# A new order of issue on every engine, without pace waits, in a fused attention, memory and MoE kernel

## The chip, the cores and the metric

One core of a Trainium2 chip runs the kernel. Its engines are TensorE (PE in the profile; PEld is its loading of weights), VectorE (DVE), ScalarE (ACT), GpSimd (POOL) and SyncE (SP, which here issues nearly all transfers). The metric is the device time of one execution in microseconds; lower is better.

## The reference

```python
B, H, S, D = (4, 8, 576, 64);  n_tokens, d_model, d_ff = (2304, 512, 1536)
scores = where(causal, -1e9, q @ k.T / sqrt(D))
a = exp(scores - max);  a /= a.sum(-1) + 1e-09
local = a @ v
q_p = phi(q)                      # phi(x) = elu(x) + 1
mem_out = (q_p @ M_prev) / (q_p @ z_prev + 1e-06)
x = sigmoid(beta) * mem_out + (1 - sigmoid(beta)) * local
xn = x / sqrt(mean(x * x) + 1e-06) * rms_g
out = (silu(xn @ w_gate) * (xn @ w_val)) @ w_out
```

The weights of the MoE part come as 8-byte floats. Products run on float16 halves (a high and a low part of each operand, three products for one), except for the first rows, which run in float32.

## The kernel before

**Tiles.** The 2304 tokens are 18 blocks of 128 rows: blocks 0 to 3 are the first of each batch (in float32, "32" in their names), then four or so full ones per batch, and two tail blocks (9 and 17) that hold the last 64 rows of two batches each. Nine chunks of two blocks go through the MoE part: `m_proj` (L1068) makes gv, the gate and value products, `m_act` and `m_split` make the hidden half-floats, `m_down` (L1142) adds into out.

**A unit of attention** is one block and a group of heads: `u_scores` (scores sc, their maxima nm and S on DVE, in one instruction for each), exp on ACT, `u_exp`'s high half of P on ACT, `u_lo` (L678) the low half on DVE and its transposing transfer PT on SP, then `u_pv` (L699), the product with v into loc. Tail blocks do the same on column halves (`tail_scores`, `tail_pv`). `x_norm` (L873) squares the finished rows x on ACT and takes the power on POOL, `x_float` (L884) and `x_split` (L899) bring x transposed into xT for gv.

**The head.** Weights (`load_w`, pieces 0 to 23) come in over SP and are converted from 8-byte floats by `f64_to_f32` (L988): two instructions on ACT (L992, L996), one on DVE (L1002). `gram` (L265) makes sums csum of k, v and of the weights, from which scales follow. gv of chunk 0 needs x0, x1 and the converted pieces.

**What sets the order.** The program is written out in Python by step lists, but the order in which each engine issues is set at the end by `issue_in_order` (L193). Each helper carries a letter (`@keep`), and its instructions are sorted into a lane for each engine and letter. `ISSUE` (L62 to 130) has one string for each of PE, ACT, DVE, POOL and SP: a letter takes the next instruction of that lane, a number behind it that many, `~k` the one k places further on. Each engine issues strictly in that order; an instruction whose operands are not ready holds all that stand behind it, and SP's transfers are issued one after the other likewise. Tiles come from pools with a fixed number of buffers, so a transfer into a pool's buffer waits until the readers of the tile that had it are done.

**Pace waits.** Besides the waits that the data need, the kernel sets waits with no data behind them (`after`, L697): the first product of each csum waits for the norm of x0 or x1 (`GDE`), the loads of kv4, kv10, kv5 and of the pre tiles for that of x1 (`GDL`), the copies for the second pair's memory likewise, the loads of w_out for earlier conversions (`paced`, L923), and both ACT instructions of pieces 2 to 11 wait for `e11`, POOL's last addition of x1 (`CDP`, `CDE`).

Of the kernel before, what the change touches and what calls it, by code (L numbers as in the profile page):

```python
# [31 lines left out]
GDE = ("x0", "x1")  # L32
GDL = ("x1", "x1")
LAG0 = 8
NA = 4
# [11 lines left out]
XP = 4  # L47
XB = 0
HLB = 5
RING = 5  # L50
PACE = 4
EARLY = 8
HTAG = ("v16", "v16", "v16", "v16")
CDP = (2, 12)
CDE = "e11"
# [78 lines left out]
def attn_memory_moe_kernel(  # L134
# [198 lines left out]
    @keep("l")  # L333
    def load_kv(n, ev=""):
# [60 lines left out]
    def stat_blk(b, i):  # L395
        if b < 2:
# [353 lines left out]
    def pair_memory(pr):  # L750
# [98 lines left out]
    def loc_evac(n, g4):  # L849
# [666 lines left out]
```

## Time and profile before

| | |
|---|---|
| runs | 627.65, 633.29, 633.80 us (median 633.29) |
| the profiled execution | 625.11 us |
| its span, from first to last instruction | 623.4 us |
| mean granted TensorE clock | 0.989 |
| PE busy | 590.9 us (95%), 6124 instructions |
| DVE, ACT, POOL busy | 433.0, 396.4, 132.9 us |
| the longest groups on PE | gv L1086 306.1, out L1160 to L1162 200.1, sc L604 78.1, gv L1079 47.5 us |
| moved by DMA | 87.57 MB, 140 GB/s on average |

Busy time is summed over the span, and matmuls overlap in the pipeline. A row of the timeline gives an instruction's start and duration; in brackets stands how long the engine had been idle before it and what released it. [...]

### The profile page before, as it was taken

Reading aid. Unit: us, or ns where it says so; the run is one execution under the profiler, and the core shown is the slowest. Engines: PE = TensorE matmul, PEld = TensorE weight load, DVE = VectorE, ACT = ScalarE, POOL = GpSimd, SP = SyncE. Lnnn points to the kernel's source line nnn. Section 1 sums busy time; section 2 is a strip of 40 time slices with the busy share of each in tenths; the row PEclk is TensorE's granted clock in tenths of the full one; section 3 lists DMA queues with packets and bytes.
Section 4 is the critical chain, followed back from the end, with each engine's and each line's share of the span. In section 5 each row is a group of like instructions: output and inputs, shape, how many; then the busy total and the mean of one; then the engine's idle time right before and its main releaser. Section 6 shows DMA issues by size and latency. Waiting matters only on the chain. (4 is left out here: it accounts for less than half of the span.)

```text
span 623.4 us, 15863 instructions
## 1 busy us (share of the span) xinstructions
PE 590.9 (95%) x6124; PEld 458.6 (74%) x6124; DVE 433.0 (69%) x1271; ACT 396.4 (64%) x856; POOL 132.9 (21%) x221
## 2 busy tenths in 40 slices
PE   5789999999999999999998999999999999989996
PEld 4768886677767888877766667777787787767774
DVE  3767689899999778776864677796876855632221
ACT  4687587998987757676565665975775644532221
POOL 2320001124332222121221221122222212121111
PEclk9979999999999999999999989999999999989999
DMA  7996246579769687885587279559996434620001
GB/s 259 359 388 262 86 148 207 144 175 201 159 99 195 132 170 121 190 156 93 74 202 118 58 161 163 133 99 155 158 152 117 87 68 99 100 44 18 34 1 35
DMA packets 183787, 87.57 MB, mean 140 GB/s; under 512 B 165792, under 2 KB 165792, under 8 KB 183712
## 3 DMA queue, kind: packets, MB, share of 16 engines
q1 hardware_dynamic: 180640, 81.82, 60.6%
q10 hardware_dynamic: 3072, 4.74, 2.5%
q8 instruction: 48, 0.79, 0.5%
q14 instruction: 27, 0.22, 0.1%
HBM read 37.77 MB, written 4.72 MB: 68 GB/s over the span
## 5 line engine op out<-in xcount | busy, mean ns | idle before, releaser
L1086 PE MATMUL gv<-xT,wgv 128*128 128x256 f16 x2304 | 306.1, 274 | 1.9 <-DMA xT<-x 1.6
L1086 PEld LDWEIGHTS <-wgv 128*128 128x128 f16 x2304 | 220.7, 98 | 44.8 <-issue 3.5
L1125 POOL TENSOR_TENSOR h<-th,h 128x256 f16<-128x256 f32 x88 | 64.2, 729 | 287.6 <-ACT h L1124 283.5
L667 ACT ACTIVATE S<-S,nm 128x256 f32<-128x256 f32 (+3 forms) x112 | 70.5, 640 | 51.4 <-DVE nm L610 32.3
L686 DVE SCALAR_TENSOR_TENSOR P<-S,P 128x512 f16<-128x512 f32 (+2 forms) x96 | 67.4, 704 | 31.0 <-ACT P L184 30.7
L1104 DVE SCALAR_TENSOR_TENSOR th<-th,gv 128x256 f32<-128x256 f32 x96 | 39.7, 414 | 63.5 <-ACT th L1103 63.3
L604 PE MATMUL sc<-kT,qT 128*128 128x128 f16 x576 | 78.1, 219 | 5.4 <-DMA kT<-row 2.0
L1103 ACT ACTIVATE th<-gv,wt 128x256 f32<-128x256 f32 x96 | 44.5, 463 | 44.2 <-PE gv L1086 39.5
L610 DVE CUSTOM_DVE_ANT_0 S<-sc,mask,qsc 128x256 f32<-128x256 f32 (+2 forms) x96 | 57.3, 610 | 19.8 <-PE sc L604 19.4
L1161 PE MATMUL out<-wo,h 128*128 128x512 f16 x176 | 67.0, 381 | 0.0
L1162 PE MATMUL out<-wo,h 128*128 128x512 f16 x176 | 66.6, 381 | 0.0
L1160 PE MATMUL out<-wo,h 128*128 128x512 f16 x176 | 66.5, 381 | 0.0
L184 ACT ACTIVATE P<-S 128x512 f16<-128x512 f32 (+2 forms) x96 | 57.8, 604 | 11.5 <-DMA PT<-P 10.8
L1124 ACT CAST h<-th 128x256 f16<-128x256 f32 x88 | 35.1, 399 | 42.8 <-DVE th L1107 38.4
L604 PEld LDWEIGHTS <-qT 128*128 128x128 f16 x576 | 48.2, 98 | 11.2 <-issue 6.9
L1079 PE MATMUL gv<-xT,wgv 128*128 128x256 f32 x192 | 47.5, 398 | 0.8 <-DVE xT L895 0.8
L1107 DVE SCALAR_TENSOR_TENSOR th<-th,wt,gv 128x256 f32<-128x256 f32 x96 | 45.7, 476 | 1.7
L724 PE MATMUL loc<-v,PT 128*128 128x65 f16 x288 | 41.1, 193 | 3.9 <-DVE t L844 1.9
L1079 PEld LDWEIGHTS gv<-xT,wgv 128*128 128x128 f32 x192 | 37.0, 199 | 8.1 <-issue 1.9
L726 PE MATMUL loc<-v,PT 128*128 128x65 f16 x288 | 41.3, 192 | 0.0
L725 PE MATMUL loc<-v,PT 128*128 128x64 f16 x288 | 40.8, 194 | 0.0
L724 PEld LDWEIGHTS <-PT 128*128 128x128 f16 x288 | 27.4, 97 | 8.4 <-DMA PT<-P 3.1
(231 smaller groups left out, 1004.6 us busy)
## 6 DMA issues: line engine op xcount, KB each, us to landing
kv<-in_qkv_dram SPq DMA_DIRECT2D x40, 256.0 KB, 3.9
q<-in_qkv_dram SPq DMA_DIRECT2D x18, 256.0 KB, 3.6
wo<-in_moe_w_out_dram SPq DMA_DIRECT2D x8, 512.0 KB, 4.0
out_dram<-res ACTq DMA_DIRECT2D x16, 256.0 KB, 2.9
wgv<-in_moe_w_val_dram SPq DMA_DIRECT2D x7, 512.0 KB, 9.2
wo<-in_moe_w_gate_dram SPq DMA_DIRECT2D x7, 512.0 KB, 8.0
qT<-qT SPq DMA_DIRECT2D x28, 128.0 KB, 2.7
wgv<-in_moe_w_gate_dram SPq DMA_DIRECT2D x5, 512.0 KB, 7.5
```

The lines of the kernel that those rows point to most:

```text
L184: got = fn(*p, **k)
L604: nc.tensor.matmul(t[:, g * w + j * P : g * w + (j + 1) * P], qT[n][:, t2, h, :], kT[blk_of[(b, j)]][:, h, :], start=(t2 == 0), stop=(t2 = ...
L610: nc.vector.tensor_tensor_reduce(out=s[:, g * w : (g + 1) * w], in0=t[:, g * w : (g + 1) * w], in1=mask[:, m0 : m0 + w], scale=qsc[n][:, 5 ...
L667: nc.scalar.activation(v_, v_, AF.Exp, bias=nm[:, g : g + 1], scale=-1.0)
L686: m = nc.vector.scalar_tensor_tensor(out=p16[:, w : 2 * w], in0=s[:, :w], scalar=PSCALE, in1=p16[:, :w], op0=ALU.mult, op1=ALU.subtract)
L724: nc.tensor.matmul(a, phi_, vhi, start=(j == 0), stop=False)
L1079: nc.tensor.matmul(o, wgv[:, 1 + p, o0 : o0 + P], xT[0][:, cc, at], start=(cc == 0), stop=(cc == NC - 1))
L1086: nc.tensor.matmul(o, lhs, xT[c][:, rhs, :], start=(cnt == 0), stop=(cnt == 3 * NC - 1))
L1125: nc.gpsimd.tensor_tensor(h16[:, 1], th, h16[:, 0], ALU.subtract)
L1160: nc.tensor.matmul(o, hh, whi, start=(f == 0), stop=False)
L1161: nc.tensor.matmul(o, hh, wlo, start=False, stop=False)
L1162: nc.tensor.matmul(o, hl, whi, start=False, stop=(f == NF - 1))
```

## The change

The five strings of `ISSUE` are replaced throughout, and the pace waits go with their names. No instruction is added, removed or changed: both programs issue the same 5878 products, the same transfers and the same operations on DVE, ACT and POOL. The products of the tail blocks stand on column halves in both. Of the strings a line each stands here.

```diff
-GDE = ("x0", "x1")
-GDL = ("x1", "x1")
...
-XP = 4
-XB = 0
...
-PACE = 4
...
-CDP = (2, 12)
-CDE = "e11"
...
-        "T8ZZ~1T8ZT4SS~1S~2S~3Zu4T4S5S~1S~2S~3T4S4u2Tu2Th4T4u4~4T2hTh3T2u4Th8ss~3ss~2ss~1s2R8G4G4~4GG~3GZG~2G3Z~1GZT4ZT4"
+        "T8ZZ~1T4ZT4SS~1S~2S~3ZT4u3T4S4TSS~1S~2S~3T3uS4T2u4h4T2u4~4T3h4T~1Tu4T3h4s2s2~2ss~1s2h4R4ss4~3s3R4ZG4G4~4G8T4Z~1Z"
...
-    def gram(acc, src, first, last, ev=""):
+    def gram(acc, src, first, last):
...
-            m = nc.tensor.matmul(acc[:, :P], w, w, start=first and g == 0, stop=last and g == 3)
-            if g == 0 and ev:
-                after(m, event[ev])
+            nc.tensor.matmul(acc[:, :P], w, w, start=first and g == 0, stop=last and g == 3)
...
-            ins = nc.sync.dma_start(out=stage[n][:, j], in_=qkv[at_row[n], :, j, :])
-            if ev:
-                after(ins, event[ev])
+            nc.sync.dma_start(out=stage[n][:, j], in_=qkv[at_row[n], :, j, :])
...
-            if b > 1:
-                after(m, event['x1'])
...
-        if p - PACE in begun:
-            tc.add_manual_dep(
-                ins.ins, begun[p - PACE].ins.name,
...
-        begun[p] = nc.scalar.activation(dst, r[:, :, 1], AF.Prelu, scale=2.0 ** -112, alpha=2.0 ** 32)
-        late = CDP[0] <= p < CDP[1]
-        if late:
-            after(begun[p], event[CDE])
...
+        nc.scalar.activation(dst, r[:, :, 1], AF.Prelu, scale=2.0 ** -112, alpha=2.0 ** 32)
```

Line numbers of the program after are lower: L950 and L951 there are L992 and L996 here, L379 is L387, L469 is L477, L684 is L692, L623 is L631, L678 is L686.

**ACT in the head,** about 25 us in. junk_369 is the square of x0, junk_401 that of x1; S with den are exponentials, wgv_84 the conversions of weights, ph_542 the first step of phi for block 2. Before:

```order
L659 ACTIVATE S_295,den_308<-S_295,nm_296 128x128 x4
L387 ACTIVATE junk_369,xs_368<-t1_0_326 128x512
L387 ACTIVATE junk_401,xs_400<-t1_1_341 128x512
L509 ACTIVATE ph_542<-q2_198 128x512
L992 ACTIVATE wgv_84<-wgv_84 128x512
L996 ACTIVATE wgv_84<-wgv_84 128x512
```

After:

```order
L651 ACTIVATE S_295,den_308<-S_295,nm_296 128x128 x4
L379 ACTIVATE junk_369,xs_368<-t1_0_326 128x512
L950 ACTIVATE wgv_84<-wgv_84 128x512 x2
L951 ACTIVATE wgv_84<-wgv_84 128x512
L950 ACTIVATE wgv_84<-wgv_84 128x512
L379 ACTIVATE junk_401,xs_400<-t1_1_341 128x512
L379 ACTIVATE junk_468,ssm0_467<-wo_85 128x512
L950 ACTIVATE wgv_84<-wgv_84 128x512
```

Four instructions of three conversions stand now between the two squares, and ph_542 comes after more of them (below the piece).

**SP around kT11,** about 320 us in. PT are transposes of probabilities for the product with v, kT and phT those of keys and of phi(q), q and kv are loads. Before:

```order
L692 DMA_TRANSPOSE PT_5128<-P16_5004 128x10x128
L477 DMA_TRANSPOSE phT11_5188<-row16_5185 128x8x128
L338 DMA kv3_5301<-in_qkv_dram 128x512
L382 DMA q13_5717<-in_qkv_dram 128x512
L692 DMA_TRANSPOSE PT_5265<-P16_5131 128x10x128
L477 DMA_TRANSPOSE kT11_4959<-row16_4956 128x8x128
L692 DMA_TRANSPOSE PT_5330<-P16_5268 128x10x128
L692 DMA_TRANSPOSE PT_5446<-P16_5334 128x8x128
```

After:

```order
L494 DMA qT11_4737<-qT11_4737 64x1024
L469 DMA_TRANSPOSE kT11_4959<-row16_4956 128x8x128
L684 DMA_TRANSPOSE PT_5128<-P16_5004 128x10x128
L684 DMA_TRANSPOSE PT_5265<-P16_5131 128x10x128
L374 DMA q12_5207<-in_qkv_dram 128x512
L469 DMA_TRANSPOSE phT11_5188<-row16_5185 128x8x128
L684 DMA_TRANSPOSE PT_5330<-P16_5268 128x10x128
L684 DMA_TRANSPOSE PT_5446<-P16_5334 128x8x128
```

kT11_4959 went from behind PT_5128, phT11, two loads and PT_5265 to a place ahead of them; the loads of kv3 now stand earlier, outside the piece.

**DVE in the last attention unit,** about 545 us in. S_9117 takes scores sc_9119 and sct_9137 and their maximum nm_9118; P16 rows make the low half of the probabilities, th rows are the MoE part, fl and t2 finish attention rows. Before:

```order
L686 SCALAR_TENSOR_TENSOR P16_9070<-S_9024,P16_9070 128x640
L631 ISA S_9117,nm_9118<-sc_9119,mask_67,qsc_7898 128x512
L631 ISA nm_9118 128x1
L858 SCALAR_TENSOR_TENSOR fl_9112<-loc17_0_8788,tcb3_6421 128x4
L641 ISA S_9117,nm_9118<-sct_9137,tmask_78,nm_9118,qsc_7898 128x128
L641 ISA nm_9118 128x1
L861 RECIPROCAL fl_9112<-fl_9112 128x4
L1104 SCALAR_TENSOR_TENSOR th_8781<-th_8781,gv91_8727 128x256
L862 TENSOR_TENSOR t2_17_9111<-loc17_0_8788,fl_9112 128x256
L1107 SCALAR_TENSOR_TENSOR th_8781<-th_8781,wt_90,gv91_8727 128x256
L686 SCALAR_TENSOR_TENSOR P16_9160<-S_9117,P16_9160 128x640
```

After:

```order
L623 ISA S_9117,nm_9118<-sc_9119,mask_67,qsc_7898 128x512
L623 ISA nm_9118 128x1
L633 ISA S_9117,nm_9118<-sct_9137,tmask_78,nm_9118,qsc_7898 128x128
L633 ISA nm_9118 128x1
L839 SCALAR_TENSOR_TENSOR fl_9112<-loc17_0_8788,tcb3_6421 128x4
L842 RECIPROCAL fl_9112<-fl_9112 128x4
L678 SCALAR_TENSOR_TENSOR P16_9070<-S_9024,P16_9070 128x640
L678 SCALAR_TENSOR_TENSOR P16_9160<-S_9117,P16_9160 128x640
```

Both rows of S_9117 now stand ahead of P16_9070, and the two P16 rows stand together.

## Rows read from the trace of the kernel before

**Rows 1.** The page, part 1: busy us of each engine, share of the span, instructions.
```profile
PE 590.9 (95%) x6124; PEld 458.6 (74%) x6124; DVE 433.0 (69%) x1271; ACT 396.4 (64%) x856; POOL 132.9 (21%) x221
```

**Rows 2.** Waits of PE: line, releaser, us in total, times, longest us.
```profile
PE tp L527 <- DMA kv<-in_qkv_dram: 5.8, 1, 5.8
...
PE loc L739 <- DMA PT<-P: 2.7, 1, 2.7
...
PE loc L724 <- DVE t L844: 1.9, 1, 1.9
PE loc L724 <- DMA PT<-P: 1.7, 3, 0.7
...
PE gv L1086 <- DMA xT<-x: 1.6, 2, 1.1
...
PE csum L271 <- DVE wgv L1002: 0.2, 1, 0.2
```

**Rows 3.** Stretches: length; busy us (instructions) by engine; clock, DMA share, GB/s.
```profile
32.43:39.26 6.83, 6.05 (x18) 4.85 (x18) 4.45 (x7) 6.83 (x15) 2.56 (x5) 0.50 1.03 393
360.11:363.52 3.41, 3.41 (x16) 1.79 (x13) 1.70 (x4) 1.64 (x4) 1.35 (x2) 0.50 1.06 134
554.67:558.08 3.41, 3.15 (x41) 2.46 (x42) 0.77 (x3) 0.40 (x1) 0.72 (x1) 0.50 0.00 0
...
334.50:338.00 3.50, 3.50 (x60) 2.89 (x60) 1.79 (x8) 1.93 (x5) 0.00 (x0) 1.00 0.10 21
...
150.00:200.00 50.00, 47.93 (x520) 37.03 (x519) 49.76 (x141) 40.40 (x86) 15.95 (x24) 1.00 0.82 151
```

**Rows 4.** Timeline of the head: start us, us, instruction, idle time before it.
```profile
26.68 1.10 PE L804 MATMUL loc<-kv,PT 128*128 128x64 f32 x8 [0.76 <-DVE t L820]
...
27.02 0.74 DVE L891 TENSOR_SCALAR diag<-ident,xs 128x128 f32<-128x128 f32 x1 [0.40 <-POOL xs L880]
...
27.62 0.62 PE L271 MATMUL csum<-kv 128*128 128x128 bf16 x8
...
29.08 0.63 ACT L387 ACTIVATE junk<-t 128x512 bf16<-128x512 f32 x1 [3.02 <-POOL t L822]
...
30.93 1.05 DVE L891 TENSOR_SCALAR diag<-ident,xs 128x128 f32<-128x128 f32 x1
...
32.03 1.75 PE L894 MATMUL xtp<-diag,t 128*128 128x128 f32 x8 [2.85 <-DVE ph L511]
...
34.56 7.32 PE L1079 MATMUL gv<-xT,wgv 128*128 128x256 f32 x22 [0.78 <-DVE xT L895]
```

**Rows 5.** Two stretches of the head, and loads of w_val (page, part 6).
```profile
0.00:20.00 20.00, 12.86 (x83) 10.58 (x83) 9.69 (x58) 11.33 (x32) 4.52 (x20) 1.00 0.83 294
20.00:30.00 10.00, 8.42 (x80) 8.09 (x79) 7.86 (x30) 5.17 (x24) 3.74 (x7) 1.00 1.05 346
...
wgv<-in_moe_w_val_dram SPq DMA_DIRECT2D x7, 512.0 KB, 9.2
```

**Rows 6.** Timeline, 325 to 335 us: SP's issues and two waits of PE.
```profile
325.84 1.38 SPq L692 DMA_TRANSPOSE PT<-P  x1
...
327.63 1.53 SPq L477 DMA_TRANSPOSE kT<-row  x1
...
328.07 0.32 PE L604 MATMUL sc<-kT,qT 128*128 128x128 f16 x2 [1.75 <-DVE nm L631]
...
334.45 0.61 PE L604 MATMUL sc<-kT,qT 128*128 128x128 f16 x8 [1.98 <-DMA kT<-row]
```

**Rows 7.** Timeline of the last attention unit, 545 to 555 us.
```profile
545.45 0.83 DVE L686 SCALAR_TENSOR_TENSOR P<-S,P 128x640 f16<-128x640 f32 x1 [1.70 <-ACT P L184]
...
546.19 0.75 DVE L631 CUSTOM_DVE_ANT_0 S<-sc,mask,qsc 128x512 f32<-128x512 f32 x1
...
546.61 2.78 PE L1086 MATMUL gv<-xT,wgv 128*128 128x256 f16 x24
...
554.93 0.26 PE L739 MATMUL loc<-v,PT 128*64 128x65 f16 x2 [2.69 <-DMA PT<-P]
```

More of the change, by code (lines that the diff above doesn't have):

```diff
@@ new lines @@
+        "sT4Zs2~3ss~2ss~1T4G8S7G4TSsTG4T2u8s~4ss~3ss~2ss~1s2~5s4s~1s2T4G4g23ZG2g4T4Zg5sG7s~3ss~2ZG3h4sT3Zs~1s2Ts3s3~1s"
+        "s2~1ss2~2ss~1s2T4G4s4s4~4G4u4h4s8g23ZSS~1S~2S~3g5g~4g3g12~1ZgS4g3TG4u4Zg16T3DG4D~1Z2D~2h4TDG4T3D2G2ZG2Dh4D~1DG16"
+        "DG7G5~1D4G7~1D2GD~1DG12D4G7S6S2~2G5S2M3~8S6G12S8DS5G2M4S2M9G10SG~12G12DG4SG20S6ZSG11ZG12S8G12P24S8G12S6G12SG12S"
+        "G12P12G12DD~2D4P4M7P8D~3DSMD2~2D2G13D2~3M3S~5GD2M3GDMSGDP8G3MS4~4P4GS~4S4GG12~3G2G2~1D~3DG4D2S5D2SD~3G2P12S6G4D"
+        "D2~2D2G4~1GS6D~3DP12G15P12D2~2D2S5G12~5GM8G4~4S2~1SG2DD~2D5D~2G8M6S3MD~2D3MD~3D2D2~1DGD~3DGP13S7P5D4P18G23D~3D5"
@@ new lines @@
+        "S3G10~1S2GS5~1SD~3P4G14S~1SPSD2~3P5D3SG12S2P7G11M2G9~1DD~2SDP3GD2~1GDSM2D~3P6MPMG2S2G3P2M2P7G5~9SG6S2GD2D~1DSG"
+        "G~1GDG2P9G4S4~5S5M3G11PD2G2~1GSP2D4G4SP2GDP3G5DSPM4S4G10SD2~1DMG10S6G4DP2G12D2~3D3P7S2G12SS~5DG6S2P7DGP2G2~5S10"
+        "G7~5G5D~2D2S2P9GD2SGS3P2G5P5DP2SS~1DD~1P9D~1DSG7SM3DP9S4G2M5DG3S2DD2~1G17P8DG~3G2PSG6DS2G2P2G2S4PG2SG6SP2SG2S3PG"
+        "MPGSGP2S2GD4MP3G14M2DG4P6MPM2SG4P7MPDS7G10~2G3SD3S~7PGDD~2S2GP10S4G2PS6~1SD~2D2G3P5D~1SG6PG6D3P4S7G18P2S~1G3S~1S"
+        "G3D~3M2S4DP11S2G4D4G2PG12MD2D2~1P24DG11SD2~1M4G7MSG2~6DGS3G3S2~3GP7D4P2S2~3G3~1D~3S~3P2S3G6~1GP5GPGD2G9S~3DG~2"
@@ new lines @@
+        "S5~3MPS3P6G3~2PMD2S2G2M3G6S3G2D~3M2G7S3~5S3G4MD2D2~1DS2G9DD3~2P11SP11D2PG16S4G19S20P12D2D2~1DG7~5S20G5P14G5DP10"
+        "G12YD~3D5P12G6M16S20G16D6G2DG11S20M16G25DP30S7P11S13P2D4G6DG6D2~2P6S20P10D4G24S10P31S10P27D5G12P3S15S4~1SG7G~5"
+        "D3~3G5D3G23S2D6S~6S6D~3D3S7G21P60DG3S5DG12DS4G11P60S7M4G10DG3D4G11M4G12~1M2G9D2D2~1D2M3G2P12D~3D2D~1GP2GMGM2G11"
+        "D2PG9PDP2~8G3P6P10~2DD3~1DG12D~3P5~2G2~12P2D2G6PSG3~6P3D3G6P3G19D2D2~1DS10DSG12D2~3D3G6S3S2~3M4~8M8S2G5S4~1GSDM4"
+        "G12DS6D~2DG12S6G12D2~1S6D~4G12P8S4PDPD~3D2D~1DG10P7S6~2PG2S3P8G4SG2PG6D4S2PDP8G11S6DG12D2YGM3D3S8DP9M4S8G5P9S2M"
@@ new lines @@
+        "S2G17P3S8P6GS2GSP9G10D2G3DG10P12D2~3SD6G13DS8M8S3D2D3~1DD~3D2S2G10G2~2S3GP5GP7DP11G10D2G23PD6P2G3P10G56D2D~1D3"
+        "P12D2G2P5SD~1S7P19S8P4DP8G15S3GM8S4DG3~8G2S5~1SG4G7~2M6G2DM2S3D2D3~1DG14D3~3D3S12P12D2~3D2D~1DS6P12G24S2G10MG2MG"
+        "S3M2GD2MGSG2G5~7M3G7DP11G4DG3D2PSP8S~5P4G5SD6S3G5P9S2~1MG3~2P5MPG5~2MPG4~2S3~1P2SG9~2G2M3G3D~3D5SP3M2G12S2P6S~3S"
+        "G12S~2DD~2D2G9P3S~2P3S2DG15P7~3P2DS~3S3G8S2PSGSGSP2D6G2S4~2S2G2SG6P7G~4G4PG2D2D3~1D2SGPDS2PG4SP2S3D~1PG4P2G2DP3"
+        "G4SD~2G2SPG3~4DG~4P3G4PS2G8DGD~2D2MP4SG6M2DG4DGMS5M4~4M4G12G2~12S6~2S2G11DG11P7D~2DD2~1DG9DD3~2G5S2P5DSP7DG5P4S"
@@ L106 @@
-        "ECAHECAECHAHNAXHAHAHAHAO2HAHAHAHAHAHAHAHAHAHAHO"
+        "fI~1IT2fT2U2ITE2E~1E3TU2E7E~2E~1ENU~6U2~2UNtU2~1fUU~7UU2~2U2U~2UtUAU2~2ATUTU~7To2AU~1UU~3fU~3E~3E3ATU4E~3EE~1E"
+        "U~6TU~4U2U~3AU3U2~2U2ATxU4Ax2U2xE2E~1EU2~2U2xcUxE~1NUE~1E2AXcU2xU4xU2cU~1xU2ANUxfXxkc2AU~1UxqAv2ckxc2UrxqUcxckcx"
+        "AFAcxqfxHrvxkE~1ExACE2HECFAO2xE~2EAHxv2ECxAE~1CHxEAEHrCEAykECyE2HyHvAyCfNEqXCyHAE~1FEyCvHvEACErHyEvyCNCyXfysAEks"
+        "C2qAyHFyHE2CrACO~1HAE~1OHECACHEfACNEXkHsAsqCECEAFHrEC2HEAHCEACECHEAfHCNEAXks2CAqEFCHEAHrCECAEHCHECOAOAECEHCHNfXA"
@@ new lines @@
+        "iUfA2U2~1uUs~1seUii~1Ufe~14i~1gZTue5UguUAZUAUA2g2g~6gg~5gg~4gg~3g~5g~1g~2g~1g2e~1eU2iTge~8xUsAxisAexgUZS4xUe3ge"
+        "e~1g~16S4U~1xUeuieg~16uxZuUTg2g~6gA2g~5gXi2g2~4igZeUg~3xig~2U~1xUTg2~5g~11g~5g~10g~5g~9g2~5g~7g~5g~6Uig~5xAg~6"
+        "g2~2Ag~3Ug~3xg~1g2fz~5XxfUA2kUq2xA2v~1qkq2vxQx~5rxx~3q4x~4xUkx~5xAFqx~2zAxA2qf2rS2vS3kA2QMM~2LM~2MxS~1S2LA2FM~1M"
+        "AZAS2zv2LSxASzLVqAqV2qzAz~1qAS2z2rzLSAykLyAVSVMQyVAMvMLAfyfMqSMXSLqAqyFAMVSqyLvVqASQLAV2SvVyVrvMLyLSyXMfMyAMAfkS"
+        "qL~1qLyqVMA2qVMqSFySLA2SrVLA2LSA2LV2MVMSMf2LA2QXkSASAq3L2SM2q2A2rSLQFALAV3MSLSLASAVLV2M2A2MSLAXAkf2SqLA2q4LSFSM2"
@@ new lines @@
+        "rLMA2V2LSA2VSLS2LA2V3LAQAM3Lf2SXA2kLS2A2LSLA2M3VLSFA2LS2V2eqS2A2e3e~1ee~1LeA2SVMSV2Le~8Mq3vqMA2S2XLMfArALQS3fSk"
+        "A2SLSkM2A2SLA2SLFLoVS3A2SVALAS2VvVALAv~1vVMVM2S2LA2q5LfrM3kA4fQV2XFV4A2q5S2rAf2XALMLSASAM~2SkQMLFMLS2A3LSMALMSA"
+        "V3LeASeLq2e2qSqe2qLSe~1QAeoAv2~1VMLMVSeMVLA2vv~1SA2LSvMLXq2fqrA2fq2LSM2LA2k2A2LFV2rQA3S2VS2AV3kLS2LM2M~1MfSXAfAS"
+        "FSq4MALSVALSqV2rA2LMSQLA2V3M3Lf2SLXA2SALAkMq4A2MSMLA2LSV2qLSFA2LSVSA2V2rVA2M3QL2Xf2A2S2LA2kSLSMA2FM2LALASA2LV3S2"
+        "LS2A2LV3S2MA2MAS2MLALXS2M2A2S2LMALS2AS2V2L2VA2V3A4XA28O"
@@ L129 @@
+        "LXLr~1rL2kFL7XL4X"
     ),
@@ L333, in load_kv @@
     @keep("l")
-    def load_kv(n, ev=""):
+    def load_kv(n):
         tag = "kvt" if is_tail[n] else "kv"
@@ L405, in stat_blk @@
                 with tc.high_priority(GP):
-                    gram(csum["kv", b, j], src[j][r], i == 0, i == NI, GDE[b])
+                    gram(csum["kv", b, j], src[j][r], i == 0, i == NI)
                 if i == NI:
@@ L767, in pair_M @@
         for t, r in ((0, slice(0, D)), (1, slice(D, 2 * D))):
-            m = nc.gpsimd.tensor_copy(pairs[b // 2][0][r, b % 2, :, t, :], m4[r, :, t, :])
-            if b > 1:
-                after(m, event['x1'])
+            nc.gpsimd.tensor_copy(pairs[b // 2][0][r, b % 2, :, t, :], m4[r, :, t, :])
         if b < 2:
@@ L821, in evac32 @@
         part = t1s[n][:, four(n, g4), :]
-        event["e%d%d" % (n, g4)] = nc.gpsimd.tensor_tensor(part, part, t2, ALU.add)
+        nc.gpsimd.tensor_tensor(part, part, t2, ALU.add)
     @keep("M")
@@ L879, in x_norm @@
         )
[L880 removed]
+        nc.gpsimd.tensor_tensor(ss, ss, mhalf[:, :1], ALU.pow)
         t1s[n] = (x, ss)
@@ L966, in load_pre @@
             t = spare(f"pre{b}_{i}_{j}")
-            ins = nc.sync.dma_start(out=t, in_=qkv[at_row[blk_of[(b, i)]], :, j, :])
-            if GDL[b]:
-                after(ins, event[GDL[b]])
+            nc.sync.dma_start(out=t, in_=qkv[at_row[blk_of[(b, i)]], :, j, :])
             pre[(b, i)].append(t)
@@ L980, in load_wo @@
         raws["o", f] = r
-        ins = nc.sync.dma_start(out=r.bitcast(I64), in_=w_out[f * P : (f + 1) * P, :])
-        paced(ins, len(pcs) + f)
-    event = {}
+        nc.sync.dma_start(out=r.bitcast(I64), in_=w_out[f * P : (f + 1) * P, :])
     @keep("U")
@@ L999, in f64_to_f32 @@
         )
-        if late:
-            after(m, event[CDE])
         nc.vector.scalar_tensor_tensor(
@@ L1248, in all_stats @@
         stat_begin(b)
-        load_kv(NA + b, GDL[b])
+        load_kv(NA + b)
         if b == 0:
-            load_kv(tails[0], GDL[b])
+            load_kv(tails[0])
         for i in range(NI + 1):
```

89 lines of the change are left out of this document (19 added, 70 removed).

## Prediction

> **What bounds the kernel now.** I read four views, from coarse to fine. The page's busy line [rows 1] shows TensorE (PE) busy for 590.9 of 623.4 us and the next engine, VectorE (DVE), for 433.0, so PE's order of work sets the time. PE's 32.5 idle us are what a new order can reach, together with the time in which PE works at half its clock. The view of waits [rows 2] tells where the idle time is: 19 rows from 5.8 to 0.2 us, 27.1 in all. 5.8 of it is the first load. The remaining 5.4 us (32.5 − 27.1) lie mostly at the end, where the last result is evacuated and written. That leaves 27.1 − 5.8 = 21.3 us of waits inside the run, and the five largest (2.9, 2.7, 2.0, 1.9, 1.7) make 11.2 of them [rows 2, 4, 6]. [...] The work itself is the same, instruction for instruction.
>
> The head. The timeline [rows 4] shows the chain that PE stands behind at 32 us: POOL adds the last half of x1, ACT squares it at 29.08, POOL makes the norm, DVE builds the diagonal at 30.93 (in 1.05 us, while ph_542's ops share DVE), and PE transposes x1 at 32.03 after 2.85 idle. The ACT row says that ACT itself stood idle for 3.02 us: the conversions of the weight pieces 2 to 11 are held by `CDE` until that same addition. Then the clock falls, and 22 gv matmuls take 7.32 us.
>
> The middle. kT11's transfer leaves SP at 327.63 and PE waits for it until 334.45 [rows 6], though its row was long made: in SP's queue it stands behind PT_5265, whose own issue at 325.84 waited for DVE.
>
> The last unit. DVE takes P16_9070's low half at 545.45 first and the maxima of the last scores only at 546.19; from there the chain through exp, low half and transfer ends at 554.93, and PE has been idle for 2.69 [rows 7].
>
> **The change, part by part.**
>
> *Pace waits removed.* They are no work; their gain is that ACT, SP and POOL run on. On ACT the 3.02 us now hold two conversions and more ahead of junk_401 (order, ACT). Those conversions still have to be done somewhere, and ACT is full from 30 to 40 us, so the gain reaches PE only through what PE waits for next.
>
> *PE, DVE and ACT at the head.* csum's eight products of kv0 (0.62 us) move into the 0.76 us wait before the second half of loc1, those of kv4 (the same kind) between the two transposes, and ph_542 leaves DVE's way (the diagonal at x0's 0.74 rather than 1.05) [rows 4]. I count 0.6 + 0.6 + 0.3 = 1.5 us; 2.85 − 0.6 − 0.3 = 1.9 us of the wait before the transpose stay. Whether the clock then still falls is open: a wait of 1.98 us at 332 was followed by a stretch at 1.00 [rows 3, 6], one of 1.94 at 357 by a stretch at 0.50 [rows 3]. I take half of the 3.0 us: 1.5. kv0's load in front of q0 on SP, and smaller waits up to 50 us: 1.0. What speaks against it: kv4's two loads and other tiles, held back until now, stand among the first eight weight pieces on SP. Through the eighth lie 7.25 MB (eight pieces of 0.5 and 3.25 of other tiles); 294 GB/s for 20 us bring 5.9, 346 GB/s the rest by 24 us, and with the 9.2 us from issue to landing of such a piece it may be some us later [rows 5]. ACT is in order, so a piece that lands after 29 would hold the norm itself. Head: **−4.0**, from +1 (a late piece) to −7 (the waits, the whole clock, all small ones).
>
> *SP and PE at 320 to 335.* DVE now takes the maxima of sc_5224 before P16_5004 and P16_5131, which removes the 1.75 us wait at 328.07 [rows 6]. kT11 now stands ahead of PT_5128 and PT_5265 (order, SP). It may leave once sc_5224 has read the buffer, and from its issue to PE's start are 334.45 − 327.63 = 6.8 us; between sc_5224 and sc_5318 PE has 6.5 us of other products in the new order (counted row by row, each at its spacing in dense work, as 24 gv in 2.78 us [rows 7]). So 0.4 us of the 1.98 stays: gain 1.6. The two PT behind it go out 1 to 2 us later, but PE reads them about 1.5 to 2 us of work later than before. Together **−3.3**; bounds 0 (kT11 then delays the PT by as much) and −3.7.
>
> *357 us.* The loc wait for t (1.9) [rows 2]: the DVE chain stands about 2.0 us earlier in its queue, PE's place 0.8 earlier, so 1.2 go; if that ends the half clock, 1.6 more. **−2.8**, bounds 0 and −3.5.
>
> *Last unit.* The scores stand 1.1 us of work earlier on PE, and DVE takes their maxima (S_9117) before P16_9070 (order, DVE). Between scores and loc PE has 9.8 us of products rather than 7.2, counted as above; the chain was 10.1 and loses the 1.2 us for which DVE was busy elsewhere: 8.9. The 2.69 wait and the 1.6 of clock behind it go: **−4.3**, bounds −1 and −4.3.
>
> *The other waits.* 21.3 − 11.2 = 10.1 us, each 0.2 to 1.7. By the places of producer and consumer in both orders nearly all gain room, a fifth to several us; but such places are no times. I take half, **−5.0**, bounds 0 and −9.
>
> *New waits.* A new order on every engine makes pairs tight that were loose: some 30 edges between engines stand with under 0.3 us of room. None can be read from the trace of before; the nearest rows are the small waits of now, 0.2 to 0.9 us each. I take **+4**, bounds 0 and +12.
>
> After the last gv the order is dense and keeps its end, so the 5.4 us stay; so do nearly all of the first 5.8.
>
> **Sum:** −4.0 − 3.3 − 2.8 − 4.3 − 5.0 + 4 = −15.4. The profiled execution took 625.11 us, so 609.7. The timed runs lie at 627.65, 633.29 and 633.8, that is 2.5 to 8.7 above it; with 6 more, the middle, 616.
>
> [...] The three stretches at 0.50 each followed a wait, while 331 to 334.5, with 1.98 us idle, was followed by 1.00 [rows 3]. [...]
>
> **Rivals.**
>
> *DVE takes the lead back* (.18). From 150 to 200 us DVE is busy 49.76 of 50 [rows 3], and PE's order there follows it. What the head gains may then be waited for again: the head's 4.0 and about 2 of the others are lost, 625.1 − 9.4 = 615.7, timed 622.
>
> *New waits as large as the old* (.14). The tight pairs cost 12 and bring back two half-clock stretches (3.3): −19.4 + 15.3 = −4, 621, timed 627; with the head's gain lost too, 631. For it: no row excludes it. Against it: the big waits have named causes and these are moved.
>
> *Slower: SP's queue* (.07). SP issues 300 transfers in one order, every kT, qT and PT transfer of the attention among them. A transfer whose source is late holds all behind it, as PT_5265 held kT11; that place cost 1.98 us on PE, and a place with a half-clock stretch behind it 1.6 more, so about 2.8 on average. Nearly all have new neighbours. Six new places of this kind between 100 and 560 us eat the 15.4 (16.8), and from ten on (28) the kernel is slower: 625.1 − 15.4 + 28 = 637.7, timed 644. Against it: such a place needs a source that is later than the needs behind it, and of the waits inside the run now, kT makes 2.0, PT 4.4 and xT 1.6, 8.0 together in seven places [rows 2, 6]. [...]
>
> [...]
>
> **Chances.** My case .56 (612 to 622 timed). Faster by over 1% (under 627; about what a measurement of this kernel can tell from no change): .56 + .18 + .05 = .79. Within 1%: the .14. Slower: .07. The range from 602 to 631 leaves out the slower case, half of the last one and the upper edge of the second, under 2 in 10.
>
> **What would show it.** In the profile after: ACT without the 3 us idle at 26 to 29 and the wait before x1's transpose near 1.9; gv1 done by 41 rather than 45; kT11's wait at about 0.4; no wait over 1 us and no stretch at half clock after 545; PE's waits inside the run at 12 to 15 us rather than 21. I am wrong if new rows of over 1 us stand in the waits between 100 and 500 us, if PE's lead at 45 us is gone at 200, if a conversion near 26 us waits for a load, or if PE's waits on transfers in the body exceed the 8.0 us of now.

## The result

| | before | after |
|---|---|---|
| median of the runs | 630.47 us (626.64 to 633.8, 4 runs) | 606.83 us (603.75 to 619.18, 4 runs) |
| profiled execution | 625.11 us | 609.22 us |
| span | 623.4 us | 607.5 us |
| PE busy | 590.9 us (95%) | 588.5 us (97%) |
| PE's waits inside the run | 21.3 us | 6.7 us |
| stretches recorded at clock 0.50, before the end | 3 | 1 |

The changed kernel is faster: the ratio is 0.9611, 95% interval 0.9506 to 0.9715. That is the forecast direction and inside the range; the forecast 616 lies 9 us too high. The ratio leaves out runs that lie over 1.5% above the fastest of their kernel, here the one of 619.18. The profiled execution came out where the sum had put it, 609.22 for 609.7, but not by the sum's terms, as the sections below show.

The page after, busy time and the clock in 40 slices (tenths), where before three slices stood below 9 (a 7 and two 8) apart from the ends:

```profile
PE 588.5 (97%) x6124; PEld 459.4 (76%) x6124; DVE 439.0 (72%) x1271; ACT 394.0 (65%) x856; POOL 131.5 (22%) x221
...
PEclk9899999999999999999999999999999999999999
```

The waits of PE after, all rows (line, releaser, us in total, times, longest). They answer to [rows 2]:

```profile
PE tp L519 <- POOL ident L275: 6.8, 1, 6.8
PE xtp L874 <- DVE diag L871: 1.7, 2, 1.0
PE gv L1039 <- DMA xT<-x: 1.6, 1, 1.6
PE loc L709 <- DVE t L825: 1.0, 2, 0.7
PE out L1113 <- ACT h L1077: 0.8, 1, 0.8
PE out L1114 <- DVE wo L209: 0.6, 2, 0.4
PE gv L1032 <- DVE xT L875: 0.5, 1, 0.5
PE gv L1039 <- DVE th L1060: 0.5, 1, 0.5
```

The wait for the first load became one of 6.8 us for the identity. The two transposes of x0 and x1 wait 1.7 in place of 2.85 [rows 4]. The waits for kT and nm [rows 6] and for the last PT [rows 7] are gone, and nothing waits for PT at all. What is left inside the run adds to 6.7 us; the wait for xT is as large as before (1.6).

Four stretches of after (length; busy us of PE, PEld, DVE, ACT and POOL with instructions; clock, DMA share, GB/s), to set beside [rows 3]:

```profile
25.93:29.34 3.41, 3.41 (x19) 3.41 (x18) 2.21 (x9) 0.37 (x3) 1.50 (x3) 0.50 1.03 381
...
150.00:200.00 50.00, 47.67 (x525) 36.52 (x522) 48.64 (x138) 40.80 (x86) 15.24 (x24) 1.00 0.74 141
...
300.00:330.00 30.00, 30.00 (x424) 22.50 (x423) 23.97 (x58) 19.69 (x37) 7.26 (x11) 1.00 0.88 148
...
500.00:560.00 60.00, 60.00 (x845) 46.04 (x842) 32.47 (x87) 25.97 (x50) 13.50 (x20) 1.00 0.38 73
```

One stretch at 0.50 is left, and PE is busy without a break from 300 to 330 and from 500 to 560.

To compare two orders, I give each product on PE a place in the work: the sum of the spacings, read from dense work in the traces, of all products that stand ahead of it in its kernel's order. Both orders have the same products, 571.6 us of them by this estimate. PE's **delay** at a place is the start of the product there minus the place. What the delay grows by over a stretch of work is what this stretch lost, to waits or to the clock. (In us. The columns behind after are the experiments told below: the changed kernel once more, the old order without pace waits, the new head and the old head, the changed kernel with products of zeros, the middle in the new order, kT11 alone moved, and the last unit in the new and in the old order.)

```text
work done  before  after  after_  order_  head_  head_  warm_  mid_  kt_    last_  last_
                          again   old     new    old    after  new   first  new    old
 10         10.2    13.6    9.0    16.1    9.5   13.5    8.0   10.3  10.2   16.0   13.2
 20         14.7    16.8   10.6    25.0   11.1   17.4    9.6   14.6  14.1   25.0   16.4
 40         18.1    17.5   11.2    27.9   11.8   20.1   10.4   18.1  16.7   28.0   17.1
200         24.3    24.0   17.5    35.1   19.0   27.0   17.8   24.9  23.4   35.2   23.0
300         26.1    25.3   19.0    36.9   20.8   28.6   19.3   26.0  25.2   37.0   24.6
310         30.7    25.5   19.2    40.7   24.2   28.7   19.5   26.1  33.5   41.3   24.8
330         35.3    27.2   20.4    44.6   28.8   30.0   20.5   28.7  36.3   45.4   26.1
500         42.0    30.1   28.2    53.1   35.7   33.6   24.6   36.0  44.4   53.2   29.4
571         46.5    30.4   28.5    57.7   40.5   33.9   24.9   39.3  47.2   53.5   30.5
```

Between the two profiled executions the delay changed by −0.6 up to 40 us of work, by −0.2 from there to 300, by −7.3 from 300 to 330, −3.8 from 330 to 500 and −4.2 after it: −16.1 in all. So in this pair the head gave nothing, and the gain lies after the middle.

### The profile page after: what moved, and what is told of

Read it like the earlier page. It is cut to its first block, busy times and chain, and to the rows that moved or that the text cites. A ratio compares the mean times of both kernels' runs of the same rounds, so it can differ in the third digit from the quotient of the medians.

```text
span 607.5 us, 15787 instructions
## 1 busy us (share of the span) xinstructions
PE 588.5 (97%) x6124; PEld 459.4 (76%) x6124; DVE 439.0 (72%) x1271; ACT 394.0 (65%) x856; POOL 131.5 (22%) x221
## 4 chain that ended last, share of the span: by engine, by line
PE 75%; DVE 10%; ACT 6%; issue 4%; DMA 4%; POOL 0%; SPq 0%; DVEq 0%; ACTq 0%; POOLq 0%
PE gv L1039 33%; PE out L1114 6%; PE out L1113 6%; PE out L1115 6%; PE gv L1032 5%; PE sc L596 4%; PE tp L519 2%; ACT junk L379 2%; PE csum L267 2%; PE sc L585 2%; PE sc L619 1%; DMA kv<-in_qkv_dram 1%; DVE S L602 1%; DVE P L678 1%; PE loc L709 1%
## 5 line engine op out<-in xcount | busy, mean ns | idle before, releaser
L1039 PE MATMUL gv<-xT,wgv 128*128 128x256 f16 x2304 | 296.0, 273 | 2.0 <-DMA xT<-x 1.6
L1039 PEld LDWEIGHTS <-wgv 128*128 128x128 f16 x2304 | 215.8, 98 | 43.3 <-issue 2.5
L678 DVE SCALAR_TENSOR_TENSOR P<-S,P 128x512 f16<-128x512 f32 (+2 forms) x96 | 67.4, 703 | 22.8 <-ACT P L180 22.1
L1114 PE MATMUL out<-wo,h 128*128 128x512 f16 x176 | 65.6, 379 | 0.2 <-DVE wo L209 0.2
L1113 PE MATMUL out<-wo,h 128*128 128x512 f16 x176 | 64.4, 379 | 0.9 <-ACT h L1077 0.8
L1115 PE MATMUL out<-wo,h 128*128 128x512 f16 x176 | 63.8, 379 | 0.0
L596 PE MATMUL sc<-kT,qT 128*128 128x128 f16 x576 | 61.1, 219 | 0.3
L596 PEld LDWEIGHTS <-qT 128*128 128x128 f16 x576 | 42.0, 98 | 10.8 <-DVE nm L602 1.5
L1032 PE MATMUL gv<-xT,wgv 128*128 128x256 f32 x192 | 45.2, 383 | 0.5 <-DVE xT L875 0.5
L1032 PEld LDWEIGHTS gv<-xT,wgv 128*128 128x128 f32 x192 | 35.4, 190 | 8.7 <-issue 2.6
L709 PE MATMUL loc<-v,PT 128*128 128x65 f16 x288 | 38.7, 193 | 1.0 <-DVE t L825 1.0
L711 PE MATMUL loc<-v,PT 128*128 128x65 f16 x288 | 39.5, 193 | 0.0
L710 PE MATMUL loc<-v,PT 128*128 128x64 f16 x288 | 39.3, 194 | 0.0
L846 POOL TENSOR_TENSOR t<-t,t 128x256 f32<-128x256 f32 x28 | 23.0, 823 | 64.2 <-DVE t L843 43.3
```

The costliest lines, as they stand in the source:

```text
L596: nc.tensor.matmul(t[:, g * w + j * P : g * w + (j + 1) * P], qT[n][:, t2, h, :], kT[blk_of[(b, j)]][:, h, :], start=(t2 == 0), stop=(t2 = ...
L678: m = nc.vector.scalar_tensor_tensor(out=p16[:, w : 2 * w], in0=s[:, :w], scalar=PSCALE, in1=p16[:, :w], op0=ALU.mult, op1=ALU.subtract)
L1032: nc.tensor.matmul(o, wgv[:, 1 + p, o0 : o0 + P], xT[0][:, cc, at], start=(cc == 0), stop=(cc == NC - 1))
L1039: nc.tensor.matmul(o, lhs, xT[c][:, rhs, :], start=(cnt == 0), stop=(cnt == 3 * NC - 1))
L1113: nc.tensor.matmul(o, hh, whi, start=(f == 0), stop=False)
L1114: nc.tensor.matmul(o, hh, wlo, start=False, stop=False)
```

## The experiments

Theory after the result: the gain is the order's and lies in the body; the pace waits cost nothing, and the new head wins nothing. Rivals: the gain comes from the pace waits; the head is worth its 4 us and something hides it. Kernels named old and new mix the two orders by one rule: what started before a given time in the trace of before stands first, in one order, and the rest behind it in the other, on all engines.

### The old order without pace waits

```diff
-GDE = ("x0", "x1")
-GDL = ("x1", "x1")
...
-CDP = (2, 12)
-CDE = "e11"
...
-            after(begun[p], event[CDE])
```

> The kernel before with its own five order strings, only without the pace waits. Theory (the gain is the order's, in the body): the pace waits cost little, the profiled span stays within 4 us of the 623.4 of before, waits inside the run at 19 to 22 us, the stall before x1's transpose somewhat shorter than 2.85, those at 326, 332, 357 and 552 us all there; ratio 0.99 to 1.005. Rival (the gain is the pace waits'): span 612 or less, ratio under 0.98.

Measured: 625.27 us median of 10 runs beside 628.62 of before, ratio 0.9977 (0.9935 to 1.0018). The pace waits are worth nothing that can be measured, and the rival falls. But its profiled execution took 636.28 us, with a delay of 27.9 us at 40 us of work where before has 18.1, and no wait that before lacks there. That run is the only one of its ten above 630 us; of before's thirteen six are. Whether the pace waits have a part in that is not shown.

### The new head, the old head

```diff
-        "T8ZZ~1T8ZT4SS~1S~2S~3Zu4T4S5S~1S~2S~3T4S4u2Tu2Th4T4u4~4T2hTh3T2u4Th8ss~3ss~2ss~1s2R8G4G4~4GG~3GZG~2G3Z~1GZT4ZT4s"
+        "T8ZZ~1T4ZT4SS~1S~2S~3ZT4u3T4S4TSS~1S~2S~3T3uS4T2u4h4T2u4~4T3h4T~1Tu4T3h4s2s2~2ss~1s2h4R4ss4~3s3R4ZG4G4~4G8T4Z~1Z"
```

(This is the start of PE's string for the new head on the old rest; the old head on the new rest is the reverse.)

> Everything that started in the first 60 us of the trace of before stands in the new order, all that started later in the old one; no pace waits. Theory (the new head wins nothing, since its first 26 us lose what the rest wins): span 621 to 625, within 1% of before, the waits at 326, 332, 357 and 552 us still there. Rival (the prediction's head term of 4 us): span 619 or less.

> The opposite: the first 60 us of the trace of before in the old order, the rest in the new one; no pace waits. Theory: as fast as the changed kernel, span 603 to 609, gv of the first rows done at about 45 us as in both, no wait over 1 us between 300 and 560. Rival (head worth 4): span 611 or more.

Measured: the new head alone 618.06 us, ratio 0.9847 (0.9723 to 0.997); the old head with the rest new 616.69, ratio 0.9791 (0.9695 to 0.9887). My theory on the head falls: the two parts are worth 1.5% and 2.1%, and together they make about the 3.9% of the whole. The head's gain must have been hidden in the profiled execution of after. The early products tell by what. The same eight sc products in the first 40 us (start us, duration, instruction), of before:

```profile
12.61 1.16 PE L593 MATMUL sc<-k,q 64*128 64x128 f32 x8
```

of after:

```profile
12.20 2.07 PE L585 MATMUL sc<-k,q 64*128 64x128 f32 x8
...
17.89 1.72 PE L585 MATMUL sc<-k,q 64*128 64x128 f32 x8
...
19.80 1.16 PE L585 MATMUL sc<-k,q 64*128 64x128 f32 x8
...
37.94 7.17 PE L1032 MATMUL gv<-xT,wgv 128*128 128x256 f32 x32 [0.47 <-DVE xT L875]
```

of the old order without pace waits:

```profile
13.10 2.07 PE L582 MATMUL sc<-k,q 64*128 64x128 f32 x8
...
22.55 2.08 PE L582 MATMUL sc<-k,q 64*128 64x128 f32 x8
...
26.63 1.81 PE L782 MATMUL loc<-kv,PT 128*128 128x64 f32 x8
...
35.03 1.00 PE L782 MATMUL loc<-kv,PT 128*128 128x64 f32 x8
...
38.20 1.11 PE L871 MATMUL xtp<-diag,t 128*128 128x128 f32 x8
...
42.01 2.08 PE L871 MATMUL xtp<-diag,t 128*128 128x128 f32 x8 [2.70 <-DVE ph L500]
```

and of the new head:

```profile
11.29 1.16 PE L582 MATMUL sc<-k,q 64*128 64x128 f32 x8
...
32.23 7.28 PE L1029 MATMUL gv<-xT,wgv 128*128 128x256 f32 x32 [0.47 <-DVE xT L872]
```

Eight of these take 1.16 us at the full clock, and 2.07 or 2.08, nearly twice that, where it is low: in the third trace the eight xtp at 42.01, in a stretch recorded at 0.50 (it begins at 41.71), take 2.08 in the same way, for 1.11 at 38.20. (The profile's clock column says 1.00 up to the clock's first record. In the trace this record, at full, stands at 11.95, 19.10, 34.89 and 10.56 us in these four; the row of 1.72 us at 17.89 in after spans it.) So by the durations TensorE begins at the low clock in these executions (in before, too, four tp take 1.11 us at 9.62 and 0.66 at 12.02), and its first rise came at 12 us in before, at 19 in after, at 35 in the third. Before, the third and four kernels below (the middle, kT11 alone, the last unit new, and the old head on the new rest) have the same order in the first 60 us; their first records stand at 11.95, 34.89, 11.95, 13.06, 35.18 and 20.09. It is therefore not the order alone that sets the time of the rise. With early rises, the delay at 40 us of work is 18.1 in before and 11.8 with the new head: the head is worth 6.3 us, and gv of the first rows is done at 39.5 (32.23 + 7.28), not at 45. With rises at 19 to 20 us in both it is worth 2.6 (20.1 for the old head on the new rest, 17.5 for after).

### One instruction at the start

In after PE starts 0.9 us later than before. Its timeline at the start:

```profile
6.04 0.16 DVE L1133 TENSOR_REDUCE ga<-rg 128x1 f32<-128x4 f32 x1 [4.85 <-DMA rg<-in_moe_rms_g_dram]
...
6.17 0.17 DVE L274 MEMSET ident<- 128x128 f32 x1
...
6.41 0.29 POOL L275 TENSOR_SCALAR_AFFINE_SELECT ident<-ident 128x128 f32<-128x128 f32 x1 [5.92 <-DVE mhalf L280]
...
6.76 1.11 PE L519 MATMUL tp<-ident,kv 128*128 128x128 f32 x4 [6.76 <-POOL ident L275]
```

DVE stands at the maximum of rg, which waits for a load, with the memset of the identity behind it; POOL needs that and PE the identity.

```diff
-".J.2f2I3."
+".4f2JI3"
```

> The changed kernel with one move on DVE: the maximum of the MoE gain (it waits for a load until 6.0 us) goes from ahead of the memset of the identity to behind the first steps of phi. Theory (the late start of the new head is this one instruction): PE starts at about 5.4 to 5.8 us rather than 6.76, span 1 to 4 us shorter than 607.5. Rival: the loss in the first 26 us is of other causes, span 606.5 to 607.5 even if PE starts earlier.

Measured: PE's first wait is down to 4.9 us, more than the theory said, yet the runs lie at 607.33 to 610.44, no faster than the changed kernel (ratio to before 0.9677, 0.9594 to 0.9761). In the profiled execution PE starts 1.9 us earlier, the rise still comes at 17.5, a stretch at 0.50 follows at 24.3, and the delay at 40 us is 17.9 for 17.5. That stretch is 6.8 us long, for 3.4 in after. The theory falls: after 40 us of work nothing is left of the early start.

### Products of zeros ahead of the first load

The first rise may be what separates runs of one program. That keeping PE busy while it would wait brings the rise earlier was my guess, not a reading from a trace. These twelve products stand first in PE's order:

```diff
+    @keep("$")
+    def warm():
+        t = ps.tile([P, 512], F32, tag="sc", name="warm")
+        for _ in range(12):
+            nc.tensor.matmul(t[:, : NI * P - P], mask[:, :P], mask[:, : NI * P - P], start=True, stop=True)
```

> The kernel before with twelve products of zeros on PE ahead of its first transpose, while it would wait for the first load (their result is not used). Theory (the clock's first rise, between 11 and 35 us after the start in the profiles so far, is what separates runs at 623 to 627 from runs at 631 to 636): with PE busy from about 1.5 us the rise comes earlier in every run, the early durations are those of the full clock, all runs lie at 621 to 627. Rival (the spread comes from elsewhere): runs at 631 to 636 remain about as frequent.

> The changed kernel with the same twelve products of zeros at the start. Theory: runs within 3 us of one another, at 600 to 606, where the changed kernel's lie at 603.75 to 619.18. Rival: a spread of 10 us or more remains.

> The twelve products of zeros and the identity's earlier memset together, on the changed kernel. Theory: PE's first transpose at about 5 us rather than 6.76, rise of the clock early, 599 to 604 in all runs, the fastest of the kernels so far. Rival: PE's early start is waited for later, no faster than with the zeros alone.

Measured: before with zeros 619.21 to 626.25 in ten runs, while before itself ran at 621.44 to 635.83 beside it, seven of thirteen above 627; the changed kernel with zeros 603.83 to 606.1; with the identity's move too 605.84 to 607.95. The first records of the full clock stand at 5.86, 5.71 and 4.46 us. In before the runs above 627 are gone and 7.0 us of spread are left of 14.4; in the changed kernel it is 2.3 us, where its runs without zeros lie 15.4 apart (603.75 to 619.18). So what the zeros change at the start is the cause of most of the spread. That a run of 631 to 636 us has a late rise is seen in the two of them that were profiled (636.28 us, rise at 34.89, and 631.97 us below, rise at 35.18); for the others it is inferred. The medians gain less than I expected: 605.57 against 606.83 for the changed kernel, whose lowest run is no lower, and 624.13 against 627.84 for before (ratio 0.9965, 0.9922 to 1.0009). A clock that is up early can fall again: in before with zeros it did at 19.5 us and stayed at 0.50 for 23.9. The identity's move is again worth nothing.

> The changed kernel once more, unchanged, timed in five rounds. Theory (the first rise of the clock differs between executions of one program): the runs spread over 10 us or more, from about 603 to 615 or above, while the one with products of zeros at the start stayed within 2.3 us; the lowest are no slower than its 603.8. Rival (619.18 was a single outlier): all runs within 4 us.

Measured: six runs from 602.16 to 615.43, median 608.86, ratio to before 0.9682 (0.9591 to 0.9773). So 619.18 was no single outlier. The profiled execution had the rise at 9.5 us and a delay at 40 us of work of 11.2: the head's gain, 6.9 us here, is in the changed kernel itself.

### The middle

> The order of before, without pace waits, except that what started between 295 and 345 us in the trace of before stands in the new order there on every engine. Theory (the prediction's step on 320 to 335 us): the waits for nm (1.5 to 1.75) and for kT11 (1.1 to 2.0) are gone, PE's delays between 300 and 310 us of its work fall from 3.4 to 4.6 us to under 1, and the later ones (320 to 330 and after 500 us of work) stay. Rival (the waits come from engines that lag from earlier): they stay at 2 us or more.

The edit puts the strings' part from 295 to 345 us in the new order, all else in the old, without pace waits. Measured: 617.92 us in its one run (before beside it 628.1); from 300 to 310 us of work the delay grows by 0.1, from 300 to 330 by 2.7, where the old order has 7.7 and before 9.2, and after 500 by 3.3. The moves at this place remove these waits by themselves; the last PT is still waited for:

```profile
PE loc L721 <- DMA PT<-P: 2.8, 1, 2.8
```

Then the one move on which the prediction's term for kT11 rested:

```diff
+k DMA_TRANSPOSE kT11_4959<-row16_4956
 L DMA_TRANSPOSE PT_5128<-P16_5004
...
 L DMA_TRANSPOSE PT_5265<-P16_5131
-k DMA_TRANSPOSE kT11_4959<-row16_4956
```

> The order of before, without pace waits, and one move on SP: kT11's transfer from behind PT_5265 to ahead of PT_5128. Theory (kT11 waits in SP's queue): PE's wait for kT11 falls from 1.1 to 2.0 us to 0.3 or less; the two PT behind it may be waited for instead, at most 0.5. Rival (kT11 is bound by the buffer that the scores before it read): the wait stays within 0.3 of 1.1.

Measured: 625.9 us in its one run (before beside it 628.1). The wait for kT11 is gone (2.0 us in before, 1.2 in the old order without pace waits), and another of 4.2 has come: the delay from 300 to 310 grows by 8.3 us (old order 3.8). The new wait of PE, the wait of SP ahead of it, and the timeline between them:

```profile
PE out L1110 <- ACT res L1087: 4.2, 1, 4.2
```

```profile
SPq L466 <- PE sct L627: 6.6, 1, 6.6
```

```profile
323.41 1.23 SPq L466 DMA_TRANSPOSE kT<-row  x1
...
328.40 0.57 SPq L329 DMA_DIRECT2D kv<-in_qkv_dram  x1
...
332.21 0.63 ACT L376 ACTIVATE junk<-kv 128x512 bf16<-128x512 f32 x1 [7.44 <-DMA kv<-in_qkv_dram]
...
333.13 0.68 ACT L1087 ACTIVATE res<-out,wos 128x512 f32<-128x512 f32 x1
```

kT11 now waits on SP for sct, a reader of its buffer (6.6 us by the view of waits), and SP issues nothing from 317.16 to 323.41. The load of kv3 stands behind it and behind PT_5128 and phT11 and is issued at 328.40, where before had it at about 323; ACT's sum of squares of it idles for 7.44 us at the head of ACT's order, the result's evacuation behind it comes at 333.13, and PE needs that buffer. Neither alternative of the expectation names this. While kT11 waits, what stands behind it in SP's order does not go out either: there is no issue in the 6 us before 323.41. The whole new order moves kv3's loads ahead of kT11 as well, and has no such wait.

### The last unit

> The order of before until 540 us of its trace, the new order from there on every engine; no pace waits. Theory (the prediction's step: the moves in the last unit themselves remove its wait): PE's delays after 500 us of its work come to 1 us or less, the wait for PT is under 0.5 us. Rival (how far DVE and ACT lag behind PE when the unit begins decides, as the opposite kernel with 0.7 us of wait suggests): the wait stays at 1.5 us or more, delays over 3 us as in before (4.5).

> The changed kernel, in which all that started after 540 us in the trace of before stands in the old order on every engine. Theory (prediction's last-unit term): the wait for PT of the last unit is back at 2.5 to 3 us, with or without a stretch at half clock behind it (1.6 us more); the sum of PE's delays after 540 us grows by 2.5 to 4.5 us over the changed kernel's 0.3. Rival (the earlier units' order is what counts): under 1 us.

Measured: with only what starts after 540 us in the new order the delay after 500 us of work grows by 0.3 us, where before has 4.5 and the old order 4.6. The theory holds: the moves there remove the wait. (Its one run took 631.97 us, before beside it 628.1: its first rise came at 35.18 us, and its delay at 40 us of work is 28.0 for 18.1.) The opposite kernel, all new but for this part, took 609.42 us in its one run, and its delay there grows by 1.1 us, not 2.5 to 4.5:

```profile
PE loc L723 <- DMA PT<-P: 0.7, 1, 0.7
```

So the unit's own moves are enough but not needed: with the new order ahead of it, only 0.7 us of the wait comes back.

## Why the prediction was right, step by step

**The bound and the sum.** PE's order was the bound, and the profiled time was foretold within 0.5 us (609.7 for 609.22). That closeness was luck: the terms were less good, and their errors cancelled.

**The head (−4.0).** In the two profiled executions it gave −0.6; with an early rise of the clock in both, −6.3 (new head) or −6.9 (the changed kernel again). The two transposes wait 1.7 us together (I forecast 1.9 before the second), and the clock does not fall behind them in those two, so the half of 3.0 that I took was all of it. The 3.0 us here, the 1.6 at 357, in the last unit and in the rival with SP's queue, and the 3.3 of the rival with new waits are estimates: about half of the 6.05, 3.41 and 3.15 us for which PE was busy in the stretches at 0.50 [rows 3]. No run shows these terms by themselves; what the runs showed is eight xtp in 2.08 us at 0.50 for 1.11 at 1.00 (the old order without pace waits). The step that failed is the start. I credited kv0's load in front of q0 with a gain, and read DVE's order only from 25 us on; there the identity stands behind a load, and PE starts 0.9 us later. And the sum had no term for the clock's first rise, which came at 19 us in this pair's after and at 12 in before: of the 3.4 us by which after lies behind at 10 us of work the identity explains 0.9. So gv of the first rows is done at 45.1 (37.94 + 7.17) and not by 41; in the changed kernel's second profile it is done at 38.9. One sign failed: ACT's 3 us of idle time at 26 to 29 did not go but now stand ahead of x0's square, behind which the conversions come:

```profile
29.33 0.63 ACT L379 ACTIVATE junk<-t 128x512 bf16<-128x512 f32 x1 [3.04 <-POOL t L803]
...
33.97 0.63 ACT L379 ACTIVATE junk<-t 128x512 bf16<-128x512 f32 x1 [1.69 <-POOL t L803]
```

Before, ACT idled 1.80 us ahead of x0's square and 3.02 ahead of x1's; in the second profile of the changed kernel it is 2.09 and 1.01. The late pieces that I feared did not show: no conversion near 26 us waits for a load.

**SP and PE at 320, and 357 (−3.3 and −2.8).** Together −6.1 forecast, −7.3 measured. The maxima on DVE and kT11 were rightly seen as the causes, and the new order has neither wait; of the 1.9 us for t 0.7 are left, as forecast, and no stretch at 0.50 follows. The reason that I gave for kT11's share was half of it: the move alone costs more than it brings. I looked at the two PT that now stand behind it, and not at the load of kv3 nor at ACT, where its reader stands ahead of the evacuation.

**The last unit (−4.3).** −4.2, and that its own moves are enough is shown. That the rest of the new order alone leaves only 0.7 us of the wait I had not foreseen.

**The other waits and the new ones (−5.0 and +4).** −1.0 forecast, −4.0 measured (−0.2 up to 300 us of work, −3.8 from 330 to 500). The term for new waits was too large in this execution: new rows are few and small (out for h, 0.8; gv for th, 0.5). In the changed kernel's second profile the first of them has grown, in the same pattern as with kT11:

```profile
377.04 0.63 ACT L379 ACTIVATE junk<-kv 128x512 bf16<-128x512 f32 x1 [2.77 <-DMA kv<-in_qkv_dram]
...
382.54 0.39 ACT L1077 CAST h<-th 128x256 f16<-128x256 f32 x1
...
382.98 0.61 PE L1113 MATMUL out<-wo,h 128*128 128x512 f16 x1 [3.63 <-ACT h L1077]
```

A sum of squares of a loaded kv stands at ACT's head until the load lands, h is late, and PE waits 3.63 us; a stretch at 0.50 of 6.8 us begins at 381.6. So this wait runs from 0.8 to 3.6 us between executions. With it the second profile gives +0.9 for this whole place (−0.2 and +1.1) where the first gives −4.0; my −1.0 lies between them. Which moves make the −3.8 from 330 to 500 no run separates.

**From the profile to the runs (+6).** This step was wrong. I took the distance of before's runs from its profile as something that the kernel has. In the main it is the time of the clock's first rise, as the runs with zeros indicate, and this was by chance early in that profile (12 us) and late in the profile of after (19 us). The median of after lies 2.4 us below its profile and not 6 above it, which makes 8.4 of the 9 us by which 616 is too high.

**The rivals.** DVE did not take the lead back: of the new head's 6.3 us at 40 us of work 5.3 are left at 200. SP's queue did turn one move into a longer wait, but only where I moved it alone. The pace waits were rightly costed at nothing.

## What to carry to other kernels

Here a transfer moved forward in its queue was paid for by what it then stood ahead of: kT11 alone took away a wait of 1.2 to 2.0 us and brought one of 4.2. So follow the transfers that it passes to their readers, and to what stands behind those readers on their engine. Compare two profiles place by place in the work, not row by row, and look at durations in the first microseconds, before a gain or a loss is put down to the change. The waits that were set for pace here were worth nothing in the order that they were set for (ratio 0.9977, 0.9935 to 1.0018).

## What the runs showed of the hardware

By the early durations TensorE starts at the low clock: in after eight sc take 2.07 us at 12.20, ahead of the clock's first record, and 1.16 at 19.80, behind it. The first rise came at 19.10 us in one execution of the changed kernel and at 9.52 in another, and between 11.95 and 35.18 in six programs whose first 60 us have the same order. In the old order without pace waits PE was busy for the whole 22 us from 12 to 34 and still at the low clock, by the durations of 2.07, 2.08 and 1.81 us above (the 1.00 in the clock's column only says that there is no record yet):

```profile
12.00:34.00 22.00, 22.00 (x102) 20.31 (x103) 11.78 (x67) 10.58 (x40) 1.98 (x4) 1.00 1.03 350
```

What sets the moment of the first rise is not shown: in this execution 22 us of busy PE did not bring it, and with products of zeros from 1.2 us on it came at 5.86, 5.71 and 4.46 us in the three profiles taken.
